# A new order table for an attention-then-MoE kernel: the same instructions, searched anew on replays in which VectorE's two-input SBUF subtraction and GpSimd exclude each other

## The chip, the cores and the metric

The kernel runs on one core of a Trainium2 chip. The metric is device time in microseconds (us) of one execution. Five queues work at the same time: TensorE (PE in the profile, with its weight loads as PEld), VectorE (DVE), ScalarE (ACT), GpSimd (POOL) and the sync queue (SP), which issues all DMAs of this kernel. Each takes its instructions strictly in the order in which they were written.

## The reference

Linear attention with a softmax-like feature map, followed by a SoLU feed-forward block with a layer norm. All is float32.

```python
# q, k, v: (8, 8, 576, 64); w_phi: (64, 128)
def phi(x):
    proj = np.einsum('bhsd,df->bhsf', x, w_phi)
    proj = proj - np.max(np.abs(proj), axis=-1, keepdims=True)
    return np.concatenate([np.exp(proj), np.exp(-proj)], axis=-1)
q_p, k_p = phi(q), phi(k)
kv = np.einsum('bhsf,bhsd->bhfd', k_p, v)
num = np.einsum('bhsf,bhfd->bhsd', q_p, kv)
den = np.einsum('bhsf,bhf->bhs', q_p, np.sum(k_p, axis=2))[..., None] + 1e-06
x = (num / den) as 4608 tokens of 512
# w_in: (512, 1024), w_out: (1024, 512), g_ln: (1024,)
h = x @ w_in
e = np.exp(h - np.max(h, axis=-1, keepdims=True))
solu = h * (e / (np.sum(e, axis=-1, keepdims=True) + 1e-09))
ln = (solu - mean(solu)) / np.sqrt(var(solu) + 1e-06) * g_ln
out = ln @ w_out
```

## The kernel before

The work is cut into steps, each a Python function that issues one to a few dozen instructions on one engine. A planner object collects them with `op(...)`: a name, an engine, the names of the steps that must stand earlier, and the buffers that the step takes and uses. There are 2827 steps. Nothing is scheduled when the kernel is built: the tuple `SEQUENCE`, from line 48 on, is a permutation of the step numbers. `order()` walks through it, hands out buffer slots first in, first out, and returns the steps in that order. Each engine thus gets its instructions in the order of the table, and a wrapper (`InOrder`, line 273) pins that order. For this reason nearly every row of the profile has the line L273, and rows are told apart by the names of tiles.

Attention comes in 16 units (two pairs of heads each). The keys of a unit are taken in five groups. TensorE projects a group (`pjk`), VectorE takes the maximum of the magnitudes (`m`) and subtracts it (`dk`), ScalarE makes the two exponentials (`ek`), GpSimd sums them up over the tokens (`zacc`). For the first three units the queries go the same way (`pjq`, `m`, `dq`), and TensorE then turns them (`dT`). For the later units GpSimd makes the low part of the queries (`hq`), TensorE projects (`pq`), VectorE turns blocks (`blk`) and takes maxima (`m`), TensorE, VectorE, GpSimd and TensorE spread the maxima (`mtp`, `mt`, `mb`, `mcp`), GpSimd subtracts them (`blk<-blk,mcol`), VectorE turns back (`pT`), and ScalarE makes the exponentials (`fq`). A `visit` step on TensorE multiplies keys by values (`kvT`) and the preceding pair's features by its key-value matrix (`num`, `den`). VectorE then makes the reciprocal of the denominator in three instructions (`dE`, `cmp`, `cmr`), the sync queue spreads it through DRAM (`rb`), and GpSimd multiplies (`xa`, `xb`).

The feed-forward block runs over 36 tiles of 128 tokens. Each tile has two halves of `h` (24 matmuls), a maximum (`nm`), an exponential and a product (`eu`), a turn (`ub`), a way through DRAM (`du`, `uTs`), a split into a high part (ScalarE, `uhs`) and a low part (VectorE, `uls`), two halves of `o` (24 matmuls), and the output (`os`). Three high-low products stand for one float32 matmul. The low part is the two-input SBUF subtraction that the title speaks of:

```python
def hi_lo_sub(eng, lo, full, hi):
    eng.tensor_tensor(out=lo, in0=full, in1=hi.bitcast(F32), op=ALU.subtract)
```

On VectorE both inputs of `uls` lie in SBUF, and so do those of `w<-w,cms`, which takes the mean off the second weight matrix (eight instructions near the start). The second weight matrix's low parts (`w_out_l`) are made by GpSimd. The second matmul of the three in `moe_o` needs only the high part, the third needs `uls`.

Of the kernel before, what the change touches and what calls it, by code (L numbers as in the profile page):

```python
# [48 lines left out]
    3, 95, 0, 2, 136, 102, 132, 7, 97, 105, 140, 98, 133, 99, 88, 89, 106, 103, 107, 137, 117, 134, 135, 8, 144,  # L49
    138, 141, 14, 90, 139, 100, 208, 108, 142, 152, 101, 148, 9, 96, 143, 104, 91, 158, 119, 10, 159, 160, 155,  # L50
    109, 110, 120, 161, 41, 145, 92, 118, 121, 93, 238, 146, 94, 209, 211, 11, 149, 122, 201, 15, 35, 124, 242,
    212, 150, 153, 163, 213, 156, 16, 123, 147, 154, 151, 17, 42, 112, 157, 239, 194, 113, 43, 246, 18, 6, 202,
    111, 114, 125, 162, 126, 173, 127, 203, 12, 164, 53, 13, 240, 115, 217, 204, 166, 116, 195, 241, 165, 223,
    174, 36, 205, 44, 196, 175, 214, 167, 37, 247, 216, 176, 45, 210, 243, 177, 300, 206, 47, 128, 197, 178, 46,
    244, 28, 198, 54, 245, 38, 215, 207, 179, 168, 199, 258, 180, 225, 55, 129, 169, 200, 308, 39, 218, 307,
    181, 19, 250, 182, 226, 254, 130, 40, 230, 21, 248, 56, 183, 131, 184, 48, 259, 185, 29, 170, 315, 260, 316,
    231, 227, 57, 49, 249, 50, 171, 30, 187, 264, 188, 51, 255, 265, 266, 261, 4, 354, 256, 232, 267, 263, 251,
    228, 269, 233, 350, 262, 539, 268, 52, 224, 476, 257, 31, 309, 186, 32, 270, 219, 58, 172, 189, 229, 220,
    272, 271, 310, 221, 59, 252, 222, 302, 311, 273, 22, 274, 60, 355, 253, 477, 275, 288, 329, 356, 285, 314,
    351, 33, 303, 419, 61, 190, 279, 312, 352, 234, 322, 313, 276, 353, 286, 277, 5, 287, 23, 301, 191, 304, 24,  # L60
    317, 282, 362, 318, 62, 278, 319, 235, 280, 283, 281, 357, 290, 284, 25, 305, 34, 236, 320, 324, 306, 237,
    331, 358, 289, 321, 439, 325, 63, 291, 429, 26, 73, 330, 366, 478, 293, 192, 421, 326, 336, 294, 332, 327,
    67, 422, 292, 337, 193, 333, 338, 373, 323, 295, 334, 359, 410, 27, 423, 74, 360, 296, 335, 370, 361, 363,
    70, 371, 339, 374, 367, 375, 372, 340, 20, 328, 379, 297, 368, 412, 376, 343, 341, 424, 377, 378, 64, 342,
    381, 380, 298, 507, 369, 420, 76, 428, 79, 382, 82, 425, 299, 384, 364, 344, 397, 413, 2077, 383, 345, 447,
    385, 2078, 398, 566, 414, 399, 71, 479, 431, 415, 72, 2079, 480, 449, 386, 77, 432, 68, 450, 416, 387, 2119,
    346, 85, 75, 417, 485, 481, 483, 482, 2080, 508, 388, 484, 2120, 347, 486, 426, 487, 411, 418, 348, 456,
    430, 400, 2081, 438, 402, 556, 401, 509, 557, 365, 2082, 538, 391, 394, 2083, 392, 451, 393, 395, 433, 78,
    396, 452, 604, 427, 488, 2121, 440, 489, 434, 69, 453, 435, 2086, 490, 436, 441, 491, 510, 457, 2087, 492,
    512, 454, 442, 349, 2098, 65, 86, 437, 605, 511, 513, 514, 443, 516, 2122, 515, 517, 458, 444, 518, 80,  # L70
    2088, 493, 540, 2089, 462, 2123, 2090, 547, 403, 2099, 2124, 83, 2125, 541, 404, 606, 666, 2128, 494, 2129,
    519, 2100, 2091, 520, 495, 405, 84, 455, 497, 445, 81, 2140, 2126, 611, 66, 609, 607, 463, 2101, 2092, 2130,
    2131, 521, 464, 87, 559, 2132, 446, 2133, 459, 406, 389, 560, 460, 684, 448, 635, 608, 610, 612, 2093, 542,
    2094, 543, 2102, 2134, 498, 2141, 407, 496, 576, 613, 2103, 522, 465, 2095, 390, 614, 544, 466, 499, 2135,
    467, 461, 468, 2104, 2136, 2107, 2084, 2108, 558, 615, 523, 636, 549, 524, 545, 469, 550, 500, 637, 546,
    575, 408, 501, 548, 2109, 2110, 2127, 2111, 470, 525, 409, 616, 567, 551, 502, 471, 2142, 2112, 568, 552,
    2085, 617, 528, 584, 553, 529, 472, 554, 640, 763, 638, 2113, 618, 561, 639, 569, 2143, 641, 555, 2114, 922,
    530, 585, 473, 526, 562, 474, 668, 563, 2096, 685, 619, 644, 564, 2144, 667, 570, 620, 565, 503, 527, 642,
    586, 475, 571, 2137, 577, 2145, 643, 669, 645, 572, 621, 2146, 573, 590, 574, 2149, 578, 622, 732, 587,
    2150, 675, 625, 588, 646, 733, 531, 734, 591, 532, 592, 579, 533, 623, 2151, 626, 670, 2152, 580, 687, 2153,  # L80
    624, 647, 2115, 671, 534, 764, 648, 593, 581, 649, 688, 672, 2154, 582, 765, 504, 2138, 676, 583, 737, 650,
    703, 735, 2116, 505, 2155, 594, 589, 595, 736, 651, 627, 2156, 596, 673, 677, 2097, 741, 738, 739, 694,
    2157, 740, 535, 2147, 652, 686, 536, 742, 743, 678, 597, 506, 794, 2105, 537, 628, 2161, 674, 2224, 2162,
    629, 689, 744, 2163, 690, 691, 653, 656, 598, 657, 766, 630, 2164, 599, 696, 745, 767, 746, 697, 2148, 600,
    679, 2165, 804, 768, 712, 2158, 812, 769, 813, 2166, 680, 601, 2225, 681, 2167, 682, 772, 698, 2170, 747,
    2226, 748, 683, 699, 692, 2171, 713, 658, 602, 2168, 693, 603, 2182, 654, 814, 700, 770, 2227, 695, 771,
    701, 631, 714, 773, 860, 705, 655, 2172, 706, 2173, 749, 718, 822, 2228, 2174, 632, 774, 2229, 2175, 659,
    2230, 796, 861, 750, 660, 702, 2233, 2159, 775, 2176, 719, 707, 708, 661, 709, 776, 710, 2177, 2245, 2183,
    797, 803, 862, 633, 720, 2184, 2234, 715, 662, 634, 832, 891, 798, 704, 716, 805, 865, 721, 799, 751, 863,
    2178, 2160, 753, 824, 2235, 752, 777, 864, 825, 722, 754, 800, 711, 723, 866, 755, 717, 724, 869, 801, 778,  # L90
    867, 2236, 2179, 802, 868, 663, 779, 892, 870, 2237, 871, 806, 940, 2238, 2106, 664, 725, 893, 2239, 2117,
    2240, 756, 665, 757, 780, 872, 758, 896, 2185, 759, 831, 840, 795, 988, 781, 873, 784, 2169, 807, 726, 2186,
    894, 727, 2241, 874, 2180, 2246, 785, 808, 2187, 809, 895, 815, 2188, 782, 816, 875, 826, 876, 786, 877,
    728, 817, 897, 810, 2247, 2191, 729, 811, 730, 833, 783, 818, 841, 2192, 819, 731, 827, 820, 924, 760, 900,
    828, 821, 898, 1019, 2248, 899, 989, 941, 901, 842, 2189, 990, 846, 2249, 2250, 2193, 761, 2194, 2195, 2196,
    878, 787, 829, 881, 830, 902, 843, 834, 2197, 993, 789, 2242, 762, 882, 2251, 790, 788, 1060, 1020, 2190,
    2198, 903, 791, 835, 1021, 904, 792, 991, 836, 2199, 1079, 959, 837, 847, 848, 992, 2118, 994, 823, 995,
    793, 1022, 996, 997, 2200, 998, 999, 925, 849, 2287, 879, 850, 2288, 2231, 943, 931, 838, 1050, 926, 2329,
    905, 2181, 880, 844, 1000, 942, 2289, 927, 839, 851, 1001, 928, 852, 944, 1023, 1002, 932, 2254, 845, 2139,
    1003, 906, 2290, 907, 2255, 929, 1004, 883, 930, 1005, 853, 2291, 2232, 1006, 2292, 2256, 2257, 2330, 2258,  # L100
    933, 2293, 884, 2259, 885, 950, 2201, 934, 2296, 908, 854, 2260, 945, 923, 886, 935, 855, 1059, 1009, 2331,
    909, 1010, 2243, 936, 2266, 946, 856, 2261, 952, 2297, 1028, 953, 2332, 912, 968, 947, 913, 1116, 937, 951,
    2294, 857, 938, 914, 1069, 1026, 1024, 858, 939, 2262, 1025, 910, 2298, 969, 1027, 2299, 2333, 911, 887,
    961, 948, 1029, 949, 859, 2334, 954, 2244, 970, 2263, 1087, 955, 1052, 888, 956, 962, 2335, 2202, 1244,
    1117, 1118, 2338, 974, 1030, 915, 2339, 1011, 889, 2308, 2252, 2309, 2203, 2253, 975, 1053, 963, 1088, 957,
    2300, 2295, 1007, 2310, 964, 2301, 958, 976, 965, 1008, 971, 2336, 966, 916, 2204, 1031, 2302, 1054, 917,
    2311, 967, 1032, 972, 1055, 1056, 973, 2303, 1123, 2312, 1119, 1121, 2304, 1120, 1147, 2340, 977, 2341, 978,
    960, 1078, 1068, 2342, 979, 2313, 980, 1033, 1122, 890, 2264, 2314, 1057, 2265, 1034, 1125, 2317, 2305,
    1148, 1124, 2318, 1126, 1127, 1035, 1036, 981, 1149, 1012, 1013, 1071, 1061, 1062, 1037, 1072, 1178, 2343,
    918, 1073, 1063, 1080, 1074, 1038, 1075, 982, 1076, 1058, 1064, 983, 2306, 2267, 2337, 2268, 1014, 1089,  # L110
    2344, 2315, 1128, 1152, 1039, 2269, 1077, 1129, 1065, 1130, 1081, 1040, 1066, 2345, 1096, 1041, 1067, 1150,
# [1156 lines left out]
```

## Time and profile before

| what | value |
|---|---|
| median of three runs | 742.18 us (741.92 to 743.12) |
| the profiled execution's own time | 742.26 us |
| its span, first to last instruction | 740.4 us |
| TensorE busy in it | 716.5 us |
| VectorE, GpSimd, ScalarE busy in it | 545.4, 485.2, 377.1 us |

The profiled execution lies 0.08 us above the median and 1.86 us above its span. Busy time is a share of the span of one engine. A wait has a row of its own, with the engine that waited, what it wanted to do, and who let it go. Rows of the timeline have a start, a duration, the engine, the line, the operation and the tiles; a number in brackets at the end is the idle time just ahead of it and what ended it.

### The profile page before, as it was taken

The numbers are of one execution on the slowest core, as the hardware profiler recorded it, in microseconds if no ns is written. First come the engines' busy times: TensorE is split into PE (matmuls) and PEld (weight loads), VectorE is DVE, ScalarE is ACT, GpSimd is POOL, SyncE is SP. The second block draws the span as 40 slices with busy tenths as digits, with TensorE's granted clock in tenths as the row PEclk, the third lists the DMA queues.
The fourth block names the chain that finished last, engine by engine and source line by source line (L and its number), as shares of the span: only waits on it lengthen the run. The fifth ranks groups of instructions, "written<-read, shape, count | busy, mean of one in ns | idle before, by whom it ended". The sixth has DMA issues, their size and how long they took to land. (4 is left out here: it accounts for less than half of the span.)

```text
span 740.4 us, 13275 instructions
## 1 busy us (share of the span) xinstructions
PE 716.5 (97%) x4671; PEld 533.0 (72%) x4671; DVE 545.4 (74%) x861; ACT 377.1 (51%) x717; POOL 485.2 (66%) x507
## 2 busy tenths in 40 slices
PE   6999989999999999999999999999999999999997
PEld 4666767677667777777777777776777677778886
DVE  6999879776768787869769687669777876627651
ACT  3795665544644563645456545535644552424231
POOL 1126799985888878777778885977757867033210
PEclk9999999999999999999999999999999999999999
DMA  7874446652845675555566555563744353511241
GB/s 225 283 239 100 133 131 167 174 156 68 212 112 146 187 212 153 159 136 162 151 172 181 149 153 156 153 191 96 209 130 133 101 161 95 158 40 57 86 150 64
DMA packets 123730, 109.96 MB, mean 149 GB/s; under 512 B 58768, under 2 KB 109968, under 8 KB 123152
## 3 DMA queue, kind: packets, MB, share of 16 engines
q1 hardware_dynamic: 123664, 109.11, 51.7%
q8 instruction: 37, 0.61, 0.4%
q14 instruction: 29, 0.24, 0.1%
HBM read 76.68 MB, written 32.39 MB: 147 GB/s over the span
## 5 line engine op out<-in xcount | busy, mean ns | idle before, releaser
L273 POOL TENSOR_TENSOR zacc<-zacc,ek 128x512 f32<-128x512 f32 (+1 forms) x78 | 107.6, 1379 | 27.4 <-ACT ek L273 23.2
L273 ACT ACTIVATE ek<-dk 128x512 f32<-128x512 f32 (+1 forms) x160 | 90.0, 585 | 51.0 <-DVE dk L273 47.8
L273 PE MATMUL o<-w_out_h,uls 128*128 128x512 f32 x264 | 104.9, 397 | 2.3 <-DVE uls L273 2.3
L273 PE MATMUL o<-w_out_h,uhs 128*128 128x512 f32 x264 | 105.3, 399 | 0.0
L273 PE MATMUL o<-w_out_l,uhs 128*128 128x512 f32 x264 | 104.3, 395 | 0.0
L273 PE MATMUL h<-win_h,mxh 128*128 128x512 f32 x288 | 92.2, 401 | 0.2 <-DVE eu L273 0.2
L273 PE MATMUL h<-win_h,mxl 128*128 128x512 f32 x288 | 90.8, 396 | 0.0
L273 PE MATMUL h<-win_l,mxh 128*128 128x512 f32 x288 | 90.7, 396 | 0.0
L273 ACT ACTIVATE fq<-pT 128x576 f32<-128x576 f32 x104 | 68.5, 679 | 40.2 <-DVE pT L273 39.8
L273 POOL TENSOR_TENSOR hq<-rawq,hq 64x1152 fp32r<-64x1152 f32 x26 | 70.3, 2704 | 6.2 <-ACT hq L273 3.4
L273 ACT ACTIVATE eu<-h,nm 128x1024 f32<-128x1024 f32 x36 | 40.1, 1113 | 66.1 <-DVE nm L273 58.7
L273 DVE TENSOR_TENSOR uls<-uTs,uhs 128x1024 fp32r<-128x1024 f32 x33 | 56.6, 1714 | 20.5 <-ACT uhs L273 19.5
L273 DVE TENSOR_REDUCE m<-pjk 128x4 f32<-128x512 f32 (+1 forms) x80 | 49.4, 620 | 28.2 <-PE pjk L273 27.7
L273 PE MATMUL num<-fq,kvf 128*64 128x288 f32 x512 | 69.2, 412 | 0.4 <-DMA kvf<-dk 0.2
L273 POOL TENSOR_TENSOR xa<-E,rb 128x576 f32<-128x576 f32 (+1 forms) x32 | 30.4, 953 | 58.0 <-DMA rb<-d 36.4
L273 PEld LDWEIGHTS h<-win_h,mxl 128*128 128x128 f32 x288 | 54.4, 189 | 13.1
L273 PE MATMUL kvT<-ek,rawv 128*64 128x256 f32 x512 | 63.8, 380 | 0.0
L273 DVE TENSOR_REDUCE nm<-h 128x1 f32<-128x1024 f32 x36 | 43.6, 1212 | 27.0 <-PE h L273 26.9
L273 PEld LDWEIGHTS h<-win_l,mxh 128*128 128x128 f32 x288 | 54.2, 188 | 13.0
L273 PEld LDWEIGHTS o<-w_out_h,uls 128*128 128x128 f32 x264 | 49.6, 188 | 16.6 <-DVE uls L273 4.9
L273 DVE TENSOR_TENSOR eu<-h,eu 128x1024 f32<-128x1024 f32 x36 | 43.7, 1214 | 23.4 <-ACT eu L273 23.1
L273 POOL TENSOR_TENSOR xl<-rawk,xh 128x256 fp32r<-128x256 f32 (+1 forms) x65 | 46.2, 714 | 21.6 <-ACT xh L273 20.9
(116 smaller groups left out, 1593.4 us busy)
## 6 DMA issues: line engine op xcount, KB each, us to landing
du<-ub SPq DMA_DIRECT2D x33, 512.0 KB, 2.9
uTs<-du SPq DMA_DIRECT2D x132, 128.0 KB, 3.2
rawq<-in_q SPq DMA_DIRECT2D x26, 576.0 KB, 4.7
rb<-d SPq DMA_DIRECT2D x64, 144.0 KB, 3.7
out<-os SPq DMA_DIRECT2D x36, 256.0 KB, 2.7
rawk<-in_k SPq DMA_DIRECT2D x64, 128.0 KB, 2.9
rawv<-in_v SPq DMA_DIRECT2D x64, 128.0 KB, 3.1
dk<-kvs SPq DMA_DIRECT2D x28, 192.0 KB, 2.2
```

Of the source, the lines that this page charges most:

```text
L273: return self.tc.keep_in_program_order(method(*args, **kwargs))
```

## The change

Only the table `SEQUENCE` changes. Every step stays, with its instructions, sizes and buffers; what changes is which step stands where, and thereby which slot of a tag a tile gets. Of TensorE's 474 steps 282 stand at another place in their queue, by 1.3 places in the mean and 10 at most; of VectorE's 671 it is 531, by 2.6 and 42 at most; of GpSimd's 343 it is 284, by 2.6 and 22 at most; of the sync queue's 665 it is 601, by 7.8 and 99 at most.

```diff
 SEQUENCE = (
-    3, 95, 0, 2, 136, 102, 132, 7, 97, 105, 140, 98, 133, 99, 88, 89, 106, 103, 107, 137, 117, 134, 135, 8, 144,
+    95, 2, 0, 3, 132, 102, 136, 7, 97, 105, 88, 98, 133, 140, 106, 99, 137, 117, 134, 14, 107, 135, 108, 144,
...
```

Three places on VectorE's queue show what such a move looks like. The first stands some 90 us into the span, where the last query group of unit 2 (`dq`) meets the first feed-forward tile (`nm`, `eu`) and the weights' centring (`w`). Before:

```order
L273 TENSOR_TENSOR dk<-pjk,m 128x512
L273 TENSOR_TENSOR w_7_476<-w_7_476,cms 128x512
L273 STREAM_TRANSPOSE blk<-pq 128x288 x3
L273 TENSOR_REDUCE m_1203<-blk 128x36
L273 TENSOR_REDUCE nm<-h 128x1
L273 TENSOR_TENSOR dq<-pjq,m 128x512
L273 TENSOR_TENSOR eu<-h,eu 128x1024
```

After, at the same place:

```order
L273 STREAM_TRANSPOSE blk<-pq 128x288
L273 TENSOR_TENSOR w_5_467<-w_5_467,cms 128x512
L273 TENSOR_TENSOR w_7_449<-w_7_449,cms 128x512
L273 TENSOR_REDUCE m<-pjq 128x4
L273 STREAM_TRANSPOSE kvs<-kvT 128x384
L273 TENSOR_TENSOR dq<-pjq,m 128x512
L273 STREAM_TRANSPOSE blk<-pq 128x288 x3
L273 TENSOR_REDUCE nm<-h 128x1
L273 TENSOR_REDUCE m_1240<-blk 128x36
L273 TENSOR_TENSOR eu<-h,eu 128x1024
```

The subtraction `dq` moved from behind `nm` to ahead of the three turns `blk`, and the long maximum over `blk` moved behind `nm`. On TensorE the projection `pjq` that `dq` reads moved eight steps later in its queue.

The second place is some 570 us into the span, where a `uls` of the feed-forward block stands beside the small maximum `mt` of unit 14. Before:

```order
L273 STREAM_TRANSPOSE dE<-den 128x288
L273 TENSOR_SCALAR cmp<-dE 128x9
L273 RECIPROCAL cmr<-cmp 128x9
L273 STREAM_TRANSPOSE pT<-blk 128x288 x2
L273 TENSOR_TENSOR uls<-uTs,uhs 128x1024
L273 TENSOR_REDUCE mt<-mtp 36x32
L273 STREAM_TRANSPOSE pT<-blk 128x288 x2
```

After:

```order
L273 STREAM_TRANSPOSE pT<-blk 128x288 x2
L273 TENSOR_TENSOR dk<-pjk,m 128x512
L273 STREAM_TRANSPOSE pT<-blk 128x288 x2
L273 TENSOR_TENSOR dk<-pjk,m 128x512
L273 TENSOR_REDUCE mt<-mtp 36x32
L273 STREAM_TRANSPOSE dE<-den 128x288
L273 TENSOR_SCALAR cmp<-dE 128x9
L273 RECIPROCAL cmr<-cmp 128x9
L273 BN_STATS bst<-eu 128x6 x2
L273 BN_AGGR mv<-bst 128x2
L273 TENSOR_TENSOR uls<-uTs,uhs 128x1024
```

The maximum `mt` now stands ahead of the three denominator instructions and of `uls`, which stood ahead of it.

The third place is some 210 us into the span, again with a `uls` and a `mt`, of unit 6. Before:

```order
L273 TENSOR_REDUCE m_2568<-blk 128x36
L273 TENSOR_TENSOR uls<-uTs,uhs 128x1024
L273 STREAM_TRANSPOSE dE<-den 128x288
L273 TENSOR_SCALAR cmp<-dE 128x9
L273 RECIPROCAL cmr<-cmp 128x9
L273 STREAM_TRANSPOSE pT<-blk 128x288 x2
L273 TENSOR_REDUCE mt<-mtp 36x32
```

After:

```order
L273 STREAM_TRANSPOSE pT<-blk 128x288 x2
L273 TENSOR_REDUCE m_2617<-blk 128x36
L273 STREAM_TRANSPOSE kvs<-kvT 128x384
L273 STREAM_TRANSPOSE dE<-den 128x288
L273 TENSOR_SCALAR cmp<-dE 128x9
L273 RECIPROCAL cmr<-cmp 128x9
L273 TENSOR_TENSOR uls<-uTs,uhs 128x1024
L273 TENSOR_REDUCE mt<-mtp 36x32
```

The denominator's three instructions moved ahead of `uls`, and `mt` now follows `uls` directly.

294 rows, old and new, of the table SEQUENCE are left out of this document.

## The prediction

> **What bounds the kernel now.** I read the page's head first, then the busy time by stage, then TensorE's own waits.
>
> ```profile
> span 740.4 us, 13275 instructions
> PE 716.5 (97%) x4671; PEld 533.0 (72%) x4671; DVE 545.4 (74%) x861; ACT 377.1 (51%) x717; POOL 485.2 (66%) x507
> ```
>
> TensorE is busy for 716.5 of 740.4 us, and the change takes no matmul away. What a new order can win lies in the 23.9 us in which TensorE idles; the other engines matter only where TensorE waits for them. In the stage view the columns are the window, its length, and busy us of PE, PEld, DVE, ACT and POOL:
>
> ```profile
> 0.00:37.00 37.00, 29.46 (x238) 20.75 (x239) 29.36 (x47) 21.44 (x41) 4.63 (x18) 1.00 0.79 254
> 37.00:148.00 111.00, 104.58 (x834) 74.79 (x834) 96.70 (x143) 72.60 (x154) 83.62 (x66) 1.00 0.56 157
> 148.00:666.00 518.00, 511.88 (x3289) 380.70 (x3286) 381.80 (x626) 261.31 (x490) 382.48 (x388) 1.00 0.53 148
> 666.00:741.00 75.00, 70.62 (x316) 56.80 (x314) 37.49 (x47) 21.74 (x34) 14.44 (x36) 0.99 0.26 88
> ```
>
> The idle time is 7.5 us in the first 37 us, 6.4 us in the next 111, 6.1 us in the long middle, and 4.4 us at the end. The start and the stretch to 148 us are dense with waits; the middle loses about 0.012 us per us. The waits of TensorE by cause (total, times, longest):
>
> ```profile
> PE pjk L273 <- DMA wph<-in_w_phi: 5.1, 1, 5.1
> PE pq L273 <- DVE mt L273: 2.5, 4, 1.0
> PE dT L273 <- DVE dq L273: 2.3, 2, 1.6
> PE o L273 <- DVE uls L273: 2.3, 3, 1.4
> PE pjk L273 <- DVE dk L273: 1.4, 1, 1.4
> PE pjq L273 <- DVE dq L273: 1.2, 1, 1.2
> PE pjk L273 <- ACT E L273: 0.9, 1, 0.9
> PE pjq L273 <- DMA rawq<-in_q: 0.9, 1, 0.9
> ```
>
> The first is the load of the first weights; three DMAs stand at the head of the sync queue in both tables, so it stays. The other rows sum to 11.5 us; they are the pool from which the gain must come.
>
> **What the exclusion costs.** Three groups of VectorE (total busy, mean ns), and the spread (minimum/median/maximum ns) of two of them:
>
> ```profile
> L273 DVE TENSOR_TENSOR uls<-uTs,uhs 128x1024 fp32r<-128x1024 f32 x33 | 56.6, 1714 | 20.5 <-ACT uhs L273 19.5 <-DMA rawk<-in_k 0.8
> L273 DVE TENSOR_TENSOR w<-w,cms 128x512 f32<-128x512 f32 x8 | 10.3, 1308 | 0.6 <-ACT cms L273 0.6
> L273 DVE TENSOR_SCALAR cmp<-dE 128x9 f32<-128x9 f32 x32 | 17.5, 546 | 1.1
> L273 DVE TENSOR_TENSOR uls<-uTs,uhs x33: 1182/1252/3710, 117.3 to 724.4; 128x1024 fp32r<-128x1024 f32 x33
> L273 DVE TENSOR_SCALAR cmp<-dE x32: 173/374/1772, 36.0 to 643.8; 128x9 f32<-128x9 f32 x32
> ```
>
> The same `uls` takes 1.18 us or up to 3.71 us: 33 x (1.714 - 1.182) = 17.6 us are lost in it. VectorE idles 195 us, so this is no bound by itself; it costs where something TensorE wants stands behind. Here is such a place, VectorE, GpSimd, TensorE in turn:
>
> ```profile
> 117.34 2.88 DVE L273 TENSOR_TENSOR uls<-uTs,uhs 128x1024 fp32r<-128x1024 f32 x1
> 117.44 1.28 POOL L273 TENSOR_TENSOR zacc<-ek 128x512 f32<-128x512 f32 x1
> 120.27 0.50 PE L273 MATMUL o<-w_out_h,uls 128*128 128x512 f32 x1 [1.36 <-DVE uls L273]
> ```
>
> GpSimd's `zacc` begins 0.10 us after `uls` and still finishes first; `uls` ends 1.50 us after it. The Trainium skill (SBUF — State Buffer, Who interferes with whom) says that a VectorE instruction with two SBUF inputs contends with a GpSimd instruction that reads SBUF, and that whoever issues first holds the port for the whole instruction. By that `uls` would have kept `zacc` out; the trace agrees on the contention (2.88 us against 1.18) and not on the right of the first here.
>
> **The change, place by place.** I follow the waits above through the new order.
>
> At 93 us TensorE waits for `dq`:
>
> ```profile
> 88.98 0.68 DVE L273 TENSOR_TENSOR w<-w,cms 128x512 f32<-128x512 f32 x1
> 89.99 1.21 DVE L273 STREAM_TRANSPOSE blk<-pq 128x288 f32<-128x288 f32 x3 [0.34 <-PE pq L273]
> 91.24 1.35 DVE L273 TENSOR_REDUCE m<-blk 128x36 f32<-128x1152 f32 x1
> 93.07 1.23 DVE L273 TENSOR_REDUCE nm<-h 128x1 f32<-128x1024 f32 x1 [0.48 <-PE h L273]
> 94.22 0.68 DVE L273 TENSOR_TENSOR dq<-pjq,m 128x512 f32<-128x512 f32 x1
> 94.95 0.88 PE L273 MATMUL dT<-ident,dq 128*128 128x128 f32 x6 [1.59 <-DVE dq L273]
> ```
>
> The new order puts `dq` ahead of the three `blk` and of `nm`, so it is ready before TensorE is through with `h`: 1.59 us go. What is late next is the maximum over `blk`, now behind `nm`: with 1.35 us after nm's end at 94.3 it is done at 95.65, just as TensorE, 1.59 us earlier, comes to `mtp`; I charge 0.2 us. Net 1.4 us, bounds 0 and 1.59.
>
> At 573 us TensorE's `pq` waits for the buffer that `mt` frees:
>
> ```profile
> 569.29 2.67 POOL L273 TENSOR_TENSOR hq<-rawq,hq 64x1152 fp32r<-64x1152 f32 x1 [0.42 <-ACT hq L273]
> 570.51 1.49 DVE L273 TENSOR_SCALAR cmp<-dE 128x9 f32<-128x9 f32 x1
> 572.34 1.30 POOL L273 TENSOR_TENSOR zacc<-ek 128x512 f32<-128x512 f32 x1 [0.38 <-ACT ek L273]
> 572.86 1.86 DVE L273 TENSOR_TENSOR uls<-uTs,uhs 128x1024 fp32r<-128x1024 f32 x1
> 574.65 0.27 DVE L273 TENSOR_REDUCE mt<-mtp 36x32 f32<-36x128 f32 x1
> 574.98 0.40 PE L273 MATMUL pq<-hq,w_hh 128*128 128x288 f32 x1 [0.97 <-DVE mt L273]
> ```
>
> `mt` stood behind two held instructions, `cmp` (it ends with GpSimd's `hq`) and `uls`. In the new order it is ahead of both. Gain 0.9 us, bounds 0 and 0.97.
>
> At 117 us the wait of 1.36 us for `uls`: between `ub` and `uls` stood a denominator, a variance and three turns; now only two turns back, a block maximum and `kvs` do, and `uls` can begin some 2 us earlier, if its data have arrived (the trace does not say: its start had no idle time ahead). Bounds 0 and 1.36; I take 1.0, nearer the upper end since more than the wait is cleared. The other two waits for `uls` (0.9 us together) I leave.
>
> The other three waits of `pq` for `mt` are 1.5 us. In two of them the new table has a half of `h` between, or no longer the pair that shares the buffer: 0.8 us of the 1.0; the third is at 215 us and is a rival's place, 0 here.
>
> `pjq` behind `dq`, 1.2 us at 57 us: VectorE is busy 87% of that stretch (96.70 of 111 us), so a place gained by one is lost by another. Bounds 0 and 1.2; half, 0.6.
>
> `pjq` behind `rawq`, 0.9 us near 23 us: that projection now stands five steps later, so its load is hidden, but the loads of those in front are then the late ones. Bounds 0 and 0.9; 0.5.
>
> One place gains less than it seems:
>
> ```profile
> 12.32 0.69 DVE L273 TENSOR_SCALAR w<-wraw 128x1024 uint32<-128x1024 uint32 x1
> 12.92 0.42 DVE L273 TENSOR_TENSOR dq<-pjq,m 128x256 f32<-128x256 f32 x1
> 13.40 0.33 PE L273 MATMUL dT<-ident,dq 128*128 128x128 f32 x1 [0.72 <-DVE dq L273]
> 16.71 0.67 PE L273 MATMUL pjk<-wph,rawk 128*128 128x256 f32 x2 [0.59 <-DMA rawk<-in_k]
> ```
>
> The weight step `w` moves behind `dq`, and 0.72 us go there, but 3 us later TensorE waits for `rawk`. Its load has moved only two places forward on the sync queue, ahead of two value loads. Where the load doesn't come sooner, TensorE only arrives earlier and waits longer. Bounds 0 and 0.72; 0.4.
>
> Sum of what goes: 1.4 + 0.9 + 1.0 + 0.8 + 0.6 + 0.5 + 0.4 = 5.6 us.
>
> **New waits.** I can't see them in the trace of before. Above they are at least nothing. At most, a step dealt anew meets the density of the middle, which an earlier table left: 6.1 us in 518, over 740 us and for the 59% of TensorE's steps that moved (282 of 474), 5.2 us. That eats nearly everything. The ones I could follow cost 0.2 us against 5.6, but I followed places that were bad before; the good ones that turn bad I did not. I take the middle, 2.6 us. 742.26 - 5.6 + 2.6 = 739.3 against the profiled execution; that one is 0.08 us above the median, so I say 739.2, where 742.18 stands now.
>
> **Rivals.**
> First, the new waits stay near their lower bound and all of the 11.5 us but some `E`, `dk` and loads go: 742.2 - 5.6, and with the 1.4 us of `dk` too, 735.2 to 736.6. For it speaks that 17.6 us of the searched-for cost are real and that the old table was blind to them; against it that the middle already loses only 1.2%. Chance 0.20.
>
> Second, nothing measurable: the new waits are within 1.5 us of what goes, 740.7 to 743.7. A search trusts its replays, and the place at 117 us shows durations that an exclusion by first come would not give. Chance 0.26.
>
> Third, slower: the denominator's `cmp` is held too, as at 570 us, and the change counts only subtractions with two inputs. 32 x (0.546 - 0.173) = 11.9 us are lost in it, at most 1.772 - 0.173 = 1.6 us in one. The place is 215 us, where the new order puts `dE`, `cmp`, `cmr` and `uls` all ahead of `mt`:
>
> ```profile
> 211.92 0.79 DVE L273 TENSOR_SCALAR cmp<-dE 128x9 f32<-128x9 f32 x1
> 215.86 0.40 PE L273 MATMUL pq<-hq,w_hh 128*128 128x288 f32 x1 [0.53 <-DVE mt L273]
> ```
>
> A held `cmp` there delays `uls`, and that `mt`, and that `pq`. With 32 such chains, two held ones without cover (3.2 us) bring the time to 742.4, no gain; from there on it decides, and three or four give 744.0 to 745.6. Chance 0.22. The Trainium skill (SBUF — State Buffer, Who interferes with whom) lists `tensor_scalar` among the operations that can take the shared port pair; the trace agrees, since `cmp` at 570.51 ends at 572.00, as `hq` does at 571.96.
>
> **How the numbers follow.** The forecast, 739.2 (736.6 to 740.7), has 0.32; with the first rival faster has 0.52, same 0.26, slower 0.22. About 0.2%, 1.5 us, is what a measurement tells from no change. The range for 8 in 10 goes from 735.2, the low end of the first rival, to 744.8, the middle of the third; below and above I leave one in ten each.
>
> **What would show it.** In the profile after: `dT` no longer waits 1.6 us for `dq` near 93 us; no `pq` waits near 573 us; the waits for `uls` fall from 2.3 to about 1.3 us; the mean of `uls` falls from 1714 ns, if the search used what it was told; TensorE's idle time in the first 148 us falls from 13.9 to about 11 us; its load wait stays 5.1 us. If the mean of `uls` falls while the idle time does not, the waits moved elsewhere, and the second rival holds. I am wrong if waits that are not in the list above (`E` copies, key-value loads, `zacc`) grow to more than 3 us.

## The result, and the profile after

The new order is slower. Its median is 748.84 us (746.14 to 749.38, six runs), against 742.05 us for the order before on the same chip (six runs): a ratio of 1.0084, 95% interval 1.0064 to 1.0105. The profiled execution took 749.38 us. Its page's head:

```profile
span 747.5 us, 13222 instructions
PE 718.9 (96%) x4671; PEld 537.1 (72%) x4671; DVE 542.4 (73%) x861; ACT 377.3 (50%) x717; POOL 483.5 (65%) x507
```

TensorE idles 747.5 - 718.9 = 28.6 us where it idled 23.9, and is busy 2.4 us longer with the same matmuls. The stages after (window, its length, busy us of PE, PEld, DVE, ACT, POOL, granted clock, DMA share, GB/s; the last window reaches beyond the end of the span):

```profile
0.00:37.00 37.00, 30.62 (x241) 21.45 (x242) 29.47 (x43) 22.24 (x44) 5.00 (x18) 1.00 0.88 281
37.00:148.00 111.00, 105.76 (x847) 75.61 (x847) 97.55 (x150) 73.07 (x152) 82.79 (x65) 1.00 0.53 150
148.00:400.00 252.00, 250.75 (x1667) 188.05 (x1663) 193.09 (x328) 133.87 (x252) 203.88 (x204) 1.00 0.56 159
400.00:500.00 100.00, 93.26 (x607) 68.10 (x607) 70.53 (x117) 50.47 (x96) 74.36 (x70) 0.97 0.51 146
500.00:666.00 166.00, 162.04 (x981) 122.67 (x980) 115.90 (x181) 75.72 (x141) 101.23 (x114) 1.00 0.48 135
666.00:760.00 94.00, 76.49 (x340) 61.25 (x338) 35.88 (x46) 21.94 (x35) 16.24 (x38) 0.99 0.21 65
```

The same cut through the middle, before:

```profile
148.00:400.00 252.00, 249.04 (x1650) 184.24 (x1647) 194.31 (x327) 134.33 (x253) 200.21 (x197) 1.00 0.57 156
400.00:500.00 100.00, 99.64 (x665) 75.08 (x664) 70.70 (x123) 51.94 (x99) 80.25 (x83) 1.00 0.59 164
500.00:666.00 166.00, 163.19 (x977) 121.38 (x976) 116.78 (x178) 75.04 (x139) 102.02 (x110) 1.00 0.44 125
```

The idle time of the first 148 us falls from 13.9 to 6.4 + 5.2 = 11.6 us, and that of the next 252 us from 3.0 to 1.3. Then comes a stretch of 100 us that idles 6.7 us where it idled 0.4, and the next one idles 4.0 instead of 2.8. TensorE's longest waits after (total, times, longest):

```profile
PE pjk L273 <- DMA wph<-in_w_phi: 4.0, 1, 4.0
PE h L273 <- DVE eu L273: 3.0, 2, 2.7
PE pq L273 <- DVE dk L273: 2.8, 5, 1.1
PE mcp L273 <- DVE blk L273: 2.5, 1, 2.5
PE pjk L273 <- ACT fq L273: 1.8, 1, 1.8
PE mcp L273 <- DVE dk L273: 1.6, 1, 1.6
PE dT L273 <- DVE dq L273: 1.4, 2, 1.1
PE o L273 <- ACT os L273: 1.0, 1, 1.0
```

The five rows behind the first load are 11.7 us, and none of them stood among the eight rows shown of before. What the search was told of did improve, since the mean of `uls` fell from 1714 to 1433 ns; the held `cmp` rose from 546 to 650 ns:

```profile
L273 DVE TENSOR_TENSOR uls<-uTs,uhs 128x1024 fp32r<-128x1024 f32 x33 | 47.3, 1433 | 30.2 <-ACT uhs L273 16.4 <-DMA uTs<-du 11.3 <-DMA vz<-in_v 1.8
L273 DVE TENSOR_SCALAR cmp<-dE 128x9 f32<-128x9 f32 x32 | 20.8, 650 | 1.1
```

Another row turned out to matter more. It is ScalarE's: how long it stood at `uhs` until the four loads `uTs` of a tile had come back from DRAM (total, times, longest), before and after:

```profile
ACT uhs L273 <- DMA uTs<-du: 34.6, 12, 6.7
```
```profile
ACT uhs L273 <- DMA uTs<-du: 68.2, 19, 13.0
```

The loads are not slower. The last of a tile's four lands 3.3 us after its issue before and 3.4 after, in the median of 33 tiles. What changed is the room: ScalarE is through with what stands ahead of `uhs` 4.2 us behind that issue before, and 2.6 us after.

To see where a lead is won or lost, I compared in the two traces at what time TensorE comes to the same amount of work (the summed lengths of the steps behind it). After minus before:

| work done, us | 40 | 140 | 380 | 500 | 600 | 720 |
|---|---|---|---|---|---|---|
| after - before, us | -0.3 | -1.7 | -5.9 | +5.1 | +2.8 | +6.8 |

The new order leads by 5.9 us at 380 us, loses 11.0 us in the next 120, and 4.0 at the end. Three places with long waits show how. The first is at 400 us; SP's, ScalarE's, VectorE's and TensorE's rows:

```profile
393.13 0.33 SPq L273 DMA_DIRECT2D uTs<-du  x1
395.94 0.46 SPq L273 DMA_DIRECT2D uTs<-du  x1
399.67 1.04 ACT L273 CAST uhs<-uTs 128x1024 fp32r<-128x1024 f32 x1 [6.82 <-DMA uTs<-du]
400.75 1.23 DVE L273 TENSOR_TENSOR uls<-uTs,uhs 128x1024 fp32r<-128x1024 f32 x1 [2.92 <-ACT uhs L273]
402.51 0.30 PE L273 MATMUL mcp<-ident,mb 128*128 128x128 f32 x1 [2.50 <-DVE blk L273]
```

The last load of tile 15 lands 3.7 us after its issue. ScalarE has stood 6.82 us, VectorE's `uls` starts only at 400.75, and a turn `blk` stands behind it; TensorE's `mcp` waits 2.5 us for that turn. The second is at 456 us, where `cmp` is held by GpSimd's back-to-back instructions; VectorE, GpSimd, TensorE:

```profile
453.74 2.63 DVE L273 TENSOR_SCALAR cmp<-dE 128x9 f32<-128x9 f32 x1
453.80 1.28 POOL L273 TENSOR_TENSOR mxl<-xa,mxh 128x512 fp32r<-128x512 f32 x1
455.05 1.29 POOL L273 TENSOR_TENSOR zacc<-ek 128x512 f32<-128x512 f32 x1
457.07 1.28 DVE L273 TENSOR_TENSOR dk<-pjk,m 128x512 f32<-128x512 f32 x2
457.90 0.30 PE L273 MATMUL mcp<-ident,mb 128*128 128x128 f32 x1 [1.55 <-DVE dk L273]
```

The third is at 613 us, where one `uls` takes 5.32 us:

```profile
606.77 1.29 POOL L273 TENSOR_TENSOR mxl<-xa,mxh 128x512 fp32r<-128x512 f32 x1
607.14 5.32 DVE L273 TENSOR_TENSOR uls<-uTs,uhs 128x1024 fp32r<-128x1024 f32 x1 [1.56 <-ACT uhs L273]
608.03 1.26 POOL L273 TENSOR_TENSOR zacc<-ek 128x512 f32<-128x512 f32 x1
609.26 2.12 POOL L273 TENSOR_TENSOR blk<-blk,mcol 128x1152 f32<-128x1152 f32 x1
616.30 0.72 PE L273 MATMUL h<-win_h,mxh 128*128 128x512 f32 x2 [2.75 <-DVE eu L273]
```

`uls` gets through 1.08 us after `blk` ends at 611.38; the `eu` that `h` wants stands behind it.

The longer busy time is the clock. Right behind the wait at 400 us TensorE is granted 0.60 of it over 4 us:

```profile
400.00:404.00 4.00, 1.50 (x8) 1.29 (x8) 3.21 (x6) 3.69 (x8) 2.40 (x3) 0.97 0.79 169
404.00:408.00 4.00, 4.00 (x16) 2.54 (x16) 1.30 (x2) 1.58 (x4) 4.00 (x4) 0.60 0.62 190
```

At 456 to 460 us it is 0.80 and at 460 to 464 us 0.77. Each time the trace has the clock at 0.50 for 3.4 us, so 1.7 us of clock are lost in each; 2.4 of the 3.4 us show as longer busy time. The order before has no such stretch in its middle; its longest wait behind the first load is the 1.59 us at 93 us.

### The profile page after: what moved, and what is told of

Same layout as the page of the kernel before. It is cut to its first block, busy times and chain, and to the rows that moved or that the text cites. A ratio compares the mean times of both kernels' runs of the same rounds, so it can differ in the third digit from the quotient of the medians.

```text
span 747.5 us, 13222 instructions
## 1 busy us (share of the span) xinstructions
PE 718.9 (96%) x4671; PEld 537.1 (72%) x4671; DVE 542.4 (73%) x861; ACT 377.3 (50%) x717; POOL 483.5 (65%) x507
## 5 line engine op out<-in xcount | busy, mean ns | idle before, releaser
L273 POOL TENSOR_TENSOR zacc<-zacc,ek 128x512 f32<-128x512 f32 (+1 forms) x78 | 102.1, 1310 | 26.6 <-ACT ek L273 21.0
L273 PE MATMUL o<-w_out_h,uhs 128*128 128x512 f32 x264 | 107.2, 406 | 1.0 <-ACT os L273 1.0
L273 ACT CAST uhs<-uTs 128x1024 fp32r<-128x1024 f32 x33 | 34.5, 1046 | 72.8 <-DMA uTs<-du 68.2
L273 DVE TENSOR_TENSOR uls<-uTs,uhs 128x1024 fp32r<-128x1024 f32 x33 | 47.3, 1433 | 30.2 <-ACT uhs L273 16.4
L273 POOL TENSOR_TENSOR blk<-blk,mcol 128x1152 f32<-128x1152 f32 x26 | 55.6, 2138 | 9.4 <-ACT mcol L273 9.4
```

The source lines that it names most:

```text
L273: return self.tc.keep_in_program_order(method(*args, **kwargs))
```

## The experiments

"New" and "old" are the two tables. Times are medians. The order before ran beside each group of kernels on the same chip (742.44, 742.66, 742.53, 743.38 and 741.60 us), and differences are taken to that. Waits are given as the profile's rows have them; some recorded expectations count the same waits up to 0.4 us longer (at 613 us 3.15 where the row has 2.75).

**First round: which half, and the held instructions.** x1 takes the first 1541 steps of the new table and the others in the old one's order; x2 the other way round.

```diff
-SEQUENCE = new
+SEQUENCE = new[:1541] + [s for s in old if s not in new[:1541]]   # x1; x2 with the two exchanged
```

> The table's first 1541 steps (to about 350 us) in the new order, all others in the old order. Theory A, the loss sits in a few places of the second half: by TensorE's progress the new table is 5.4 to 5.9 us ahead of the old one at that point, so 742.05 - 5.4 = 736.6 us (735.5 to 738). Rival B, the lead is repaid later whatever stands there (the work is only dealt otherwise): about 742. Rival C, the slower time is that of the chip's clock or of the loads, spread over the whole: about 745.

> The complement: the first 1541 steps in the old order, all others in the new order. Theory A: the new table loses 6.8 + 5.4 = 12.2 us against the old one after that point, so 742.05 + 12.2 = 754 us (751 to 756). Rival B: the loss belongs to the lead, and without the lead it doesn't come: 742 to 745. Rival C: about 745.

x1: 742.88 us, ratio 0.9995 (0.9971 to 1.0019). x2: 754.86 us, 1.0175 (1.0127 to 1.0223). x2 came out as theory A said, so the loss is in the second half of the new table. x1 did not: it lies where rival B put it. The lead of its first half, 2.7 us at 340 us, didn't reach the end, since at the seam TensorE waited 2.52 us for a `blk`, and the clock was halved behind it. In x2 ScalarE stood 65.0 us at `uhs`, as in the new order, in x1 32.0, as in the old one.

x3 moves the `uls` of tile 15 back behind the turns, so that the place at 400 us goes. y1 leaves out `cmp`, the addition of 1e-6.

```diff
 # x3, VectorE's order
-uls(15), blk, blk
+blk, blk, uls(15)
 # y1
-nc.vector.tensor_scalar(out=c, in0=flat[:, ::32], scalar1=EPS, scalar2=None, op0=ALU.add)
-nc.vector.reciprocal(out=st["cmr", sub], in_=c)
+nc.vector.reciprocal(out=st["cmr", sub], in_=flat[:, ::32])
```

> The new table with one step moved: the uls of feed-forward tile 15 goes behind the two turns blk that stand behind it near 400 us; all buffers stay the same. Theory A: TensorE's wait of 2.7 us for those turns goes, and the stretch of halved clock right behind it (some 3.4 us at half speed, 1.6 us lost) goes with it: 748.8 - 4.3 = 744.5 us. Rival: the wait goes and the low clock is of another cause: 746.2. Rival: another step is late in its place: 748.

> The new table with the addition of 1e-6 to the denominators left out, so that the 32 instructions cmp are gone and the reciprocal reads dE itself. Theory D, held cmp instructions make the waits at 456 us (1.7 + 0.6 us) and 482 us (1.4 us): these go, and the halved clock near 460 us (1.6 us) with them: 748.8 - 5.3 = 743.5 us (742 to 745.5). Rival: the hold passes on to the next instruction that meets GpSimd, and the time stays at 747 to 749.

x3: 753.18 us (746.05 to 754.39; two of its five runs took under 747), not the 744.5 to 748 expected. The wait for `blk` at 400 us went (0.53 us for `uls` is left there), but the other waits stayed, and its profile, of the 754.39 us run, has the clock halved at 98, 460 and 617 us. y1: 744.37 us, ratio 1.0012 (0.9984 to 1.0040), in the range of the theory of the held `cmp`. The stretch from 400 to 500 us gains 3.2 us:

```profile
400.00:500.00 100.00, 96.48 (x641) 71.42 (x640) 68.94 (x120) 50.98 (x97) 76.50 (x75) 1.00 0.57 157
```

Taken alone, y1 would have closed the case on `cmp`.

**Second round: the control.** y2 is the old order without `cmp`. x4 is the new order with the product `eu` of tile 28 ahead of the `uls` that is held at 607 us.

```diff
 # x4, VectorE's order
-uls(26), bst, bst, mv, m, eu(28)
+eu(28), uls(26), bst, bst, mv, m
```

> The old order, with the denominator's cmp left out (1e-6 is not added). Theory D (the held cmp is what separates the two orders: under the old one a long cmp stands before little that TensorE wants): the gain is at most the 0.97 us of the one wait at 573 us in which a held cmp stood, and a few tenths of E copies, 740.5 to 742.4 us, so that the difference between the orders without cmp, 744.4 less this, is 2 to 4 us where it was 6.8. Rival (cmp costs both orders alike, about 4.5 us, and what separates them is elsewhere): 737 to 738.5 us.

> The new order with one step moved: the product eu of tile 28 stands ahead of the uls of tile 26, which GpSimd held for 5.3 us. Theory D (the 3.15 us wait at 613 us is lost time of its own): that wait goes, 745.5 to 746.3 us. Rival (the time comes back, since what follows is bound by loads and by the end of the queue): the wait goes, but those at 631, 651 and 718 us grow by as much, 748 to 749.5 us.

y2: 738.56 us, 0.9945 (0.9927 to 0.9963). The old order gains 4.1 us, as much as the new one's 4.5. So `cmp` costs time (the edit takes away the instruction as well as its hold), but it is not what separates the two orders: without it they are still 6.0 us apart. Theory D falls. The two savings come at different places: in the stretch from 400 to 500 us the new order idles 3.2 us less without `cmp`, the old one 0.3 us more. x4: 749.77 us, 1.0104 (1.0082 to 1.0127). The wait at 613 us went, but another came at 230 us, long before the moved step. ScalarE and TensorE in x4:

```profile
231.93 1.04 ACT L273 CAST uhs<-uTs 128x1024 fp32r<-128x1024 f32 x1 [4.12 <-DMA uTs<-du]
232.88 0.39 ACT L273 COPY E<-num 128x288 f32<-128x288 f32 x1
233.33 0.38 PE L273 MATMUL pjk<-wph_h,xh 128*128 128x256 f32 x1 [2.80 <-ACT E L273]
```

and ScalarE at the same place in the new order's own trace, where TensorE waited 0.1 us:

```profile
228.20 1.05 ACT L273 CAST uhs<-uTs 128x1024 fp32r<-128x1024 f32 x1 [1.42 <-DMA uTs<-du]
229.15 0.39 ACT L273 COPY E<-num 128x288 f32<-128x288 f32 x1
```

The order is the same up to here. The four loads of tile 5 took 3.9 us in the mean to land in one trace and 6.5 in the other (5.5 in that of n3, below). Where ScalarE stands at `uhs` for them, this jitter goes straight into TensorE, since the copy `E` that frees its bank stands behind. This gave theory F.

z1 and z2 were to take the exclusion out of both orders, with `uls` as a one-input reciprocal and no `cmp`.

```diff
-nc.vector.tensor_tensor(out=lo, in0=full, in1=hi.bitcast(F32), op=ALU.subtract)
+nc.vector.reciprocal(out=lo, in_=hi.bitcast(F32))
```

> The old order without the exclusion: the subtraction uls is replaced by a reciprocal with one input from SBUF (the low part is a wrong number), and cmp is left out. The mean of uls falls from 1714 ns to near its shortest if one input is not held. Theory D: the waits for uls (2.3 us), for mt at 573 us (1.0) and some of the rest go, 738 to 740.5 us. Rival (what VectorE is held by is covered anyway): 741.5 to 742.5 us.

> The new order without the exclusion, changed in the same way. Theory D (held instructions make the new waits): the waits at 456, 482 and 613 us go, and what stays is the wait for fq at 95 us and that at 400 us, where the data of uls come late from DRAM: 741 to 744 us, within 4 us of the old order without the exclusion. Rival (the new order is slower for reasons of its own, loads and ScalarE): the difference of 6.8 us stays, 745 us or more.

911.69 and 903.75 us: they tell nothing of the question, since a reciprocal of 1024 elements takes 6.5 us and VectorE became the bound.

**Third round: the way through DRAM.** n1 (old) and n2 (new) make the transfers as before, but `uhs` and `uls` read a constant, so nobody waits for them. `uls` still has two inputs in SBUF, so the exclusion stays.

```diff
-M["turned", t] = M["uT", t].rearrange("p a k j -> p k a j")
+M["turned", t], full = (win_h[:, i, :].bitcast(F32).rearrange("p (a k j) -> p k a j", a=4, k=8) for i in range(2))
-nc.scalar.copy(out=M["uh", t].rearrange("p k (a j) -> p k a j", a=4), in_=M["turned", t])
+nc.scalar.copy(out=M["uh", t].rearrange("p k (a j) -> p k a j", a=4), in_=full)
```

> The old order, with the way through DRAM still made, but not waited for: uhs and uls read a constant (two rows of the first weight matrix) in place of uTs, so the feed-forward output is wrong. Theory F (the new order is slower since it leaves ScalarE standing at uhs for uTs, 68 us in all where it was 35 under the old order, with E copies, fq and the uls of VectorE behind it): here little is to be had, 740 to 742.5 us. Rival G (the two orders differ in many small waits, none of them this one): 741 to 742.5 us too; only the difference to the new order, next, tells the two apart.

> The new order, changed in the same way. Theory F: ScalarE's 68 us of idle time before uhs go, and with them the waits at 400 us (2.7), about 456 and 482 us in part, and the long waits behind which the clock is halved: 741 to 743.5 us, less than 2.5 us above the old order so changed. Rival G: the difference stays, 5 us or more, 746 to 748.5 us.

n1: 740.55 us, 0.9969 (0.9947 to 0.9991). n2: 742.35 us, 0.9999 (0.9978 to 1.0019). The wait is worth 2.0 us to the old order and, from 748.84, 6.5 to the new one; the two come within 1.8 us. Theory F holds, rival G falls. But the time does not come back at the first two places. n2 idles 6.9 us from 400 to 500 us, as much as the new order:

```profile
400.00:500.00 100.00, 93.08 (x621) 69.16 (x621) 72.64 (x119) 48.09 (x91) 72.70 (x69) 1.00 0.54 149
```

Other waits have taken their place there, of 1.0 to 1.7 us, none with a halved clock behind it. What n2 gains by its profile is 2.9 us of TensorE's busy time (716.0 against 718.9), 3.0 us of idle time from 500 to 666 us, and 0.9 us behind that.

n3 mends the new order at six steps of this kind; c1 is a candidate on y2.

```diff
 # n3: ScalarE's uhs of tiles 14, 15, 20, 28 and VectorE's uls of 15, 20, each 1 to 3 places back, e.g.
-uhs(15), ek, xh
+ek, xh, uhs(15)
 # c1: y2, and
-blk, blk, blk, m, nm, dq
+blk, blk, blk, m, dq, nm
-hq, E
+E, hq
-wraw, fq
+fq, wraw
```

> The new order, with six steps moved back by one to three places in their queue, past steps that were ready: the uhs of tiles 14, 15, 20 and 28 on ScalarE, and the uls of tiles 15 and 20 on VectorE. Theory F (these waits of uhs are what costs): the wait at 400 us goes, and those up to 460 us get shorter, 744 to 746 us. Rival G (any place that is mended gives its time to the next one, as with x3 and x4): 748 to 751 us.

> A candidate: the old order without cmp (738.56 us), with three steps moved at the three longest waits of its trace: dq of unit 2 ahead of nm (a wait of 1.75 us at 92 us), a copy E of unit 4 ahead of hq, which waits for its load (1.93 us at 192 us), and a fq of unit 1 ahead of a weight step (1.14 us at 44 us). If the time at such a place is the kernel's: 735 to 737 us. If it comes back at the next place: 738 to 739.5 us.

n3: 749.59 us (743.48 to 753.73), 1.0090 (1.0062 to 1.0119). The wait at 400 us went, but the others stayed (1.7 us at 461, 2.8 at 618, 1.9 at 233), and its runs spread over 10 us, outside what theory F expected: moving six steps doesn't free the order from the transfers, for which ScalarE still waited 54.5 us. c1: 738.50 us, 0.9934 (0.9911 to 0.9957), the same as y2: the 1.59 us at 94 us became 0.68, and a new wait of 1.40 us stood 3 us behind it.

**Fourth round: do the two causes add, and does a slower transfer hurt the new order more?** n4 (new) and n5 (old) join the edits of y1 and n2. d1 (old) and d2 (new) cut each load of `uTs` into two.

```diff
+for a in (0, 2):
-    out=M["uT", t][32 * b : 32 * b + 32].rearrange("p a k j -> p a (k j)"), in_=src[:, :, b, :]
+    out=M["uT", t][32 * b : 32 * b + 32, a : a + 2].rearrange("p a k j -> p a (k j)"), in_=src[:, a : a + 2, b, :]
```

> The new order without cmp, and with uhs and uls reading a constant in place of uTs (wrong output). Theory F with the held cmp as a second cause: the two savings of the new order (4.5 and 6.5 us) add nearly, 737 to 739.5 us, within 1.5 us of the old order so changed. Rival G (a remainder that neither explains): 3 us or more above the old order so changed, 740 us or more.

> The old order, changed in the same way. The two savings (4.1 and 2.0 us) add: 736 to 737.5 us, by both theories. If they are the same time counted twice: 738.5 us.

> The old order, with each load of uTs cut into two of half the bytes: the sync queue issues eight in place of four for a tile, about 0.43 us each, so that the last lands some 1.7 us later. Theory F (the old order has some room before uhs): slower by 0.5 to 2 us, 743 to 744.5 us. Rival (the room does not matter, each such us is seen by TensorE alike): the same loss as the new order.

> The new order, changed in the same way. Theory F (ScalarE stands at uhs for uTs at 19 tiles, so a later landing is a later E, fq and uls): slower by 3 to 7 us, 752 to 756 us, at least 2 us more than the old order loses. Rival: the same loss as the old order, within 1 us.

| difference to the order before, us | as it is | no cmp | no DRAM wait | neither | loads split |
|---|---|---|---|---|---|
| new | +6.8 | +1.9 | -0.2 | -6.1 | +24.0 |
| old | 0 | -4.1 | -2.0 | -8.3 | +10.7 |
| new - old | 6.8 | 6.0 | 1.8 | 2.2 | 13.2 |

n4 took 737.32 us (0.9920, 0.9895 to 0.9944), n5 735.07 (0.9897, 0.9869 to 0.9925), d1 754.11 (1.0151, 1.0101 to 1.0200), d2 767.33 (1.0321, 1.0271 to 1.0372). The savings add in both orders, and a little more than add (12.9 us where 4.9 and 7.0 make 11.9, 8.3 where 4.1 and 2.0 make 6.1); n5 came out below its range. A remainder of some 2 us stays that neither explains, between the 1.5 of theory F and the 3 of rival G and hardly beyond the spread of the runs (n5's go from 733.08 to 739.34 us). In the profiles of n4 and n5 it lies between 400 and 500 us (4.4 us idle against 0.6). Two waits of n4 make up most of that, and ahead of one of them ScalarE stands at `hq` for another load, `rawq`:

```profile
443.44 1.15 ACT L273 CAST hq<-rawq 128x1152 fp32r<-128x1152 f32 x1 [6.19 <-DMA rawq<-in_q]
445.46 0.29 PE L273 MATMUL mtp<-ident,m 128*36 128x128 f32 x1 [1.59 <-ACT E L273]
453.20 0.37 PE L273 MATMUL pq<-hq,w_hh 128*128 128x288 f32 x1 [2.59 <-DVE dk L273]
```

n5 never stands there for more than 2.1 us. No run takes this wait away, so it is a candidate and not shown. The split loads cost far more than I expected in either order: 10.7 us in the old one and 17.2 in the new one (24.0 less 6.8), 6.5 us more, as theory F has it in sign. This is not the price of `uhs` alone: the 132 added issues also make the other transfers late, and `num` waits 5.4 us for `kvf` in d1 and 3.4 in d2.

**Fifth round: in which tiles.** p1 takes the wait away from tiles 13 to 20 alone (those of the stretch from 400 to 500 us), p2 from all the others.

```diff
+if 13 <= t <= 20:        # p2: if not 13 <= t <= 20
+    M["turned", t], full = <as in n2>
```

> The new order, with uhs and uls reading a constant in place of uTs in tiles 13 to 20 alone (wrong output). Theory F1 (the waits of uhs at 400, 438 and 476 us are what costs, with the halved clock behind them): 743 to 745 us. Theory F2 (that stretch loses as much for another reason, and only the clock's share comes back): 745.5 to 747.5 us.

> The new order, with uhs and uls reading the constant in all tiles but 13 to 20. Theory F1: 747 to 748.5 us. Theory F2 (the uls held for 5.3 us at 607 us, 3.0 us of TensorE's time, the tail's 1.0 and 0.9 before 148 us): 743.5 to 745.5 us.

p2: 743.59 us, 1.0007 (0.9988 to 1.0026), as F2 said: 5.2 of the 6.5 us come from the other tiles. Its rows from 400 us on:

```profile
400.00:500.00 100.00, 93.58 (x618) 68.69 (x618) 71.02 (x119) 50.80 (x96) 74.29 (x70) 0.98 0.53 148
500.00:666.00 166.00, 165.49 (x995) 125.14 (x994) 111.41 (x180) 77.00 (x143) 106.49 (x119) 1.00 0.47 137
666.00:760.00 94.00, 71.81 (x321) 57.77 (x319) 36.02 (x46) 20.61 (x33) 13.09 (x32) 0.99 0.19 59
```

From 500 us to the end of its span of 741.9 us p2 idles 0.5 + 4.1 us, against 4.0 + 5.0 of the new order; the third place, at 613 us, is gone. There the `uls` of tile 26 now begins 0.11 us ahead of GpSimd's `mxl`, and it is `mxl` that is held (2.32 us, where it took 1.29 in the new order):

```profile
605.57 1.30 DVE L273 TENSOR_TENSOR uls<-win_h,uhs 128x1024 fp32r<-128x1024 f32 x1 [1.09 <-ACT uhs L273]
605.68 2.32 POOL L273 TENSOR_TENSOR mxl<-xa,mxh 128x512 fp32r<-128x512 f32 x1
```

In the new order `uls` began 0.37 us behind `mxl`, and ScalarE had stood 0.37 us at its `uhs` for the load, so a wait of that size is enough to decide whether this `uls` takes 1.3 or 5.3 us. Between 400 and 500 us p2 still idles 6.4. p1: 752.43 us, 1.0128 (1.0101 to 1.0156), slower than the new order itself and outside both theories. In its profile 3.8 us are lost before 80 us of work, ahead of every place that it changes, and it idles 7.3 us from 400 to 500 us, though `uhs` waits for nothing there. Why it is slower, no run shows. Taken together, n2, p1 and p2 say that the loss from 400 to 500 us does not hang on this wait.

## Why the prediction was wrong

The step that failed is the size of the new waits. They were put at 2.6 us, between 0.2 and 5.2, from the density that the old order had reached in its middle. They are 12.7 us, lost clock included: the lead of 5.9 us at 380 us, close to the sum of the predicted gains, and the 6.8 us by which the run is late. What the density left out is the room that the order leaves between a load's issue and its reader (4.2 us in the old order, 2.6 in the new one): 5.0 of the 6.8 us go when nobody waits for `uTs`.

- **What goes, 5.6 us: right in sum, partly by luck.** The lead at 380 us is 5.9 us. Idle time in the first 148 us fell to 11.6 us, about the 11 named as a mark; but 1.0 of these 2.3 us is the wait for the first load, which is 4.0 us where 5.1 was to stay, so the places there gave 1.3 us where 3.9 were summed up for them. Another 1.7 us went from 148 to 400 us, where the sum holds 0.5 at most. The mean of `uls` fell as named, the waits of `o` for it fell from 2.3 to 0.8 us, and the wait at 573 us is gone.
- **At 93 us, 1.4 us: not kept.** `dT` there no longer waits for `dq`, but 3 us later `pjk` waits 1.8 us for the `fq` that follows from `dT`. I had named the block maximum as what is late next, and it was ScalarE.
- **New waits.** The bound of 5.2 us assumed that a table found by a search is at worst as dense everywhere as the old middle was (6.1 us in 518). The same middle idles 11.9 us now, and the longer busy time from the halved clock, which the sum had no term for, adds 2.4.
- **The list to trust.** I said I was wrong if waits off the list (`E` copies, loads, `zacc`) grew by over 3 us. They did, though not the ones that I named. What grew were waits for `eu`, `dk`, `blk` and `fq`, and behind a good part of them a transfer: the profile of before had ScalarE at `uhs` for 34.6 us, and I hadn't looked at that engine's waits at all, since ScalarE was busy only 51%.
- **The third rival, slower by held `cmp`s.** Its sign was right, with a chance of 0.22, and the mechanism is real: 4.1 and 4.5 us. But in total it costs both orders alike. Near 215 us, the place that I named, the rows after show no wait; held `cmp`s (2.63 and 2.19 us) stand ahead of the waits at 456 and 482 us.
- **"The exclusion costs where something TensorE wants stands behind"** held up: the longest new wait, 2.75 us, stands behind the `uls` at 607 us, which came to the port 0.37 us behind GpSimd.

What the runs show of the cause: 5.0 of the 6.8 us are the wait for the way through DRAM (6.8 less 1.8; without `cmp` 3.8, 6.0 less 2.2). The intervals of the four runs leave an uncertainty of some 2.5 us on that, by my estimate. Some 2 us, in the stretch from 400 to 500 us, stay open, and so does p1.

## What to carry to other kernels

When a table is searched anew, read the waits of every engine that stands between a transfer and the bound, however little it is busy: an order that leaves less room before a load's arrival pays for it in idle time, in jitter and in the clock. Run the control too: taking `cmp` out of the new order alone fitted a theory that the same edit in the old order refuted. The version that beats both is the old order without `cmp` (738.56 us, ratio 0.9945): every exponential with the flipped sign is at least 1, so a denominator is at least 128 x 576 = 73728, and 1e-6 is lost in a float32 of that size.

## What the runs showed of the hardware

- Who gets the port. In the traces of before and after, a waiting `uls` found its way in each of the 11 times that GpSimd's next instruction came 60 to 90 ns after the one before; where the next followed back to back, VectorE lost 8 of 13 times. So one `uls` of 1.18 us took 5.32 behind three GpSimd instructions, two of which began after it. At 117 us, too, a GpSimd instruction (`w_out_l`, 116.19 to 117.47 us) was at work when `uls` began; the prediction's rows do not show it. So `uls` was second there, and the trace speaks against the right of the first only in that the `zacc` behind `w_out_l` got in ahead of a `uls` that already waited.
- The halved clock follows short waits, and not always. In these traces it comes in stretches of 3.41 us, or twice that. Behind the wait of 1.79 us at 95 us, which all kernels that begin with the new order have, it came in x1, x3, x4, n3 and d2, and not in the new order, y1, n2, n4, p1 and p2; the wait of 2.75 to 2.78 us at 613 us left the clock at 1.00 in the new order, n3 and p1, and in x3 it was halved. The Trainium skill (TensorE: Matmul & The Clock Gate, Part 1: The HAM clock gate) has a window of about 3.4 us that runs freely, and the lower clock after at least one idle window. The length of the stretches agrees with that window; that 1.79 us of idle time are enough does not agree with a whole idle window.
- The same four loads of 128 KB landed in 3.9, 5.5 and 6.5 us in the mean in three traces, at a place up to which the order is the same.
- A reciprocal on VectorE takes 6.5 us for 1024 elements a partition and 0.22 us for 9.
